# Fused attention, feed-forward and routed experts on one core: the first expert's gather split by the last tile, the last routes moved ahead, six experts ranked instead of five

## The chip, the cores and the metric

One core of a Trainium2 chip. The metric is the device time of one execution in microseconds. PE is the matrix engine, DVE the VectorE, ACT the ScalarE, POOL the GpSimd, SP the engine that issues most DMAs.

## What is computed

```python
attn_out = _attn_ref(...)             # q, k, v: 4 x 12 x 448 x 64, q and k normalised
x = attn_out.transpose(0, 2, 1, 3).reshape(1792, 768)
h = x @ w_in                          # 768 -> 2048
x = (max(h, 0) + alpha * min(h, 0)) @ w_out          # 2048 -> 768
do_compute = x @ w_skip > 0           # second stage: 8 experts, one per token
e_idx = argmax(x @ w_gate); gate_w = softmax(x @ w_gate)[e_idx]
for e in range(8):                    # w1[e]: 768 x 1024, w2[e]: 1024 x 768
    y[e_idx == e] = gate_w * (max(x @ w1[e], 0) @ w2[e])
out = x; out[do_compute] += y
```

## The kernel before

Every product is made of float16 pairs (a high and a low part: three products stand for one), so each float32 matrix that comes from DRAM is cut into a high half (ACT, line 1394) and a low half (DVE, line 1401, or POOL, lines 1404 and 1408).

**Stages.** Attention runs over 24 pairs of heads. Its rows go into blocks of tokens (two 128-token tiles in most, one in block 1 and in the last, block 7); `layer1` makes 2048 columns of a block (lines 1028 to 1030), `layer2` brings them back to 768 (lines 1116 to 1118), copies a tile out of PSUM as `zt` (line 1133) and writes it to `out` (line 1155) and to the DRAM buffer `zd` (line 1158). Each tile's router scores pick an expert; `route` counts and gives each token a slot of its expert. The scores of a tile come out of nine more columns of layer 2, or out of `logits_apart` (line 1231). When the last tile is routed, `all_slots` has for each expert the list of its token rows.

**Experts.** An expert's pass has a fixed number of slots, its entry in `WIDTHS`. The first `FIXED` experts have one by their number; the others are ranked by their counts on the chip, and the expert of a rank gets that rank's width. `fetch` gathers an expert's rows out of `zd` by an indirect DMA on POOL (line 1460), in two parts (128 rows and the rest) where the width is over 128; `turns` turns them on PE (line 1476) and cuts them (lines 1480 and 1483); `ups` and `downs` are the two products (lines 1443 to 1445); `backs` turns the result back (line 1524), adds it times the gate to the gathered rows (line 1530), and a scatter on POOL writes them to `out` (line 1536). `braid` lays the order of PE out by hand: up 0, up 1, down 0, up 2, down 1 and so on. Turns of expert e stand between the down products of expert e - 2, back turns of expert e between the up products of expert e + 2. Tokens beyond a width go to a loop at the end (line 1817), which runs zero times when all fit.

**Order and buffers.** The class `Plan` simulates the engines while the program is built: `op(key, (engine, ns, step), after, takes, uses)` gives a step its priority (lower first), its duration for the planner and its place in the order of its engine's queue. On the chip each queue keeps that order. A `buf` of a pool is a place; the takes of a pool go round its places in turn. Activations of the layers live in pool `x` (4 places), rows of the experts in `rows` (4 places).

**Weights of the experts.** 16 matrices of 1024 x 768, in 12 pieces of 256 KB (w1) or 8 of 384 KB (w2), each through a staging place. The first matrices are loaded during the layers; from `GATE` (matrix 4, piece 4) on a load waits for expert 0's gather. Before, seven staging places serve matrices 0 to 5, and eight the others. Of matrix 6 and later every fourth piece (`LO_G`) has its low half made by POOL in two steps, a scaling (line 1404) and a subtraction (line 1408).

Of the kernel before, what the change touches and what calls it, by code (L numbers as in the profile page):

```python
# [206 lines left out]
def attention_moe_routed_experts(  # L207
# [42 lines left out]
    FIXED = 3  # L250
    WIDTHS = [CAP] * FIXED + [CAP, 128, 96, 80, 64]
# [8 lines left out]
    zd = dram.tile([NT, DM], F32, name="zd")  # L260
# [31 lines left out]
    big = ctx.enter_context(tc.tile_pool(name="big", bufs=4))  # L292
    gp = es_l.enter_context(tc.tile_pool(name="gp", bufs=1))
    xp = es_l.enter_context(tc.tile_pool(name="xp", bufs=N_X))
# [58 lines left out]

    def late_constants():

        make_identity(nc, ident)
# [10 lines left out]
        V.tensor_copy(tokz, tokz_i)  # L367
        pref_i = stage.tile([128, NE], I32, tag="st", name="pref_i")
# [640 lines left out]

    def layer1(blk, prev):  # L1010
# [5 lines left out]
        gs = slice(AT_G[blk], AT_G[blk] + size)  # L1016
        for m0 in range(0, KF, step):
            b_h, b_gf = buf("h"), buf("gf")
            w = {}
            for m in range(m0, m0 + step):  # L1020
                for x in range(2):
                    def mm(m=m, x=x, w=w, m0=m0):
# [11 lines left out]
                        20000 + 1000 * blk + m, ("T", 23 + 9 * size * 5 // 12, mm), takes=[b_h] if new else [],  # L1034
# [16 lines left out]
            def hi(e, w=w, at=at):  # L1051
                def f():
                    if e is A:
                        A.activation(g_h[:, at, gs], w["gf"], AF.Copy)  # L1054
                    else:
                        V.tensor_copy(g_h[:, at, gs], w["gf"])
                return f

            def lo(e, w=w, at=at):
                def f():  # L1060
                    e.tensor_tensor(g_l[:, at, gs], w["gf"], g_h[:, at, gs], op=ALU.subtract)  # L1061
# [21 lines left out]
    lgs, n_kept = {}, []  # L1083
    lgz = const.tile([128, sum(SIZES_B[:Z_LOGITS]) // 128, NL], F32, name="lgz") if Z_LOGITS else None

    def layer2(blk, done, apart, early):
# [4 lines left out]
        if early:  # L1091
            for s in range(tiles):
                n = logits_apart(t0 + s, s, done, key)
# [5 lines left out]
        for s, half, g in todo:  # L1099
            tt = t0 + s  # L1100
            if g == 0 and half == 0:
                zt[s] = ({}, buf("zt1"))
# [6 lines left out]
            def mm(g=g, w=w, half=half, n=n, s=s):  # L1109
# [4 lines left out]
                for kk in range(4 * g, 4 * g + 4):  # L1114
                    gh, gl = (x[:, kk, AT_G[blk] + s * 128:AT_G[blk] + (s + 1) * 128] for x in (g_h, g_l))
# [7 lines left out]
                + ([n_router] if n > HD else []),  # L1123
# [6 lines left out]
            def z_out(w=w, half=half):  # L1130
                if half == 0:
                    w["zt"] = ztp.tile([128, DM], F32, tag="zt", name="zt")
# [6 lines left out]
            w["n_out"] = n_out  # L1139
            if half == 0:  # L1140
# [16 lines left out]
            def keep(w=w, tt=tt):  # L1157
                Y.dma_start(out=zd[tt * 128:(tt + 1) * 128, :], in_=w["zt"])
# [61 lines left out]
    def logits_apart(tt, s, done, key):  # L1220
        b_z = buf("z")
        w = {}
        o = AT_G[FROM_B.index(128 * tt)] if 128 * tt in FROM_B else 128 * s

        def mm():
# [3 lines left out]
            for kk in range(KF):  # L1229
                gh, gl = (x[:, kk, o:o + 128] for x in (g_h, g_l))  # L1230
# [13 lines left out]
    counted = [None, None]  # L1244

    def route(tt, n, late=[]):
# [30 lines left out]
        def position():  # L1277
# [6 lines left out]
            lgs[tt]["sel"] = sel  # L1284

# [40 lines left out]
        counted.append(n8)  # L1326

    reads = {}
    for blk in range(NB):
        done = layer1(blk, reads)  # L1330
        read = layer2(blk, done, blk < max(1, Z_LOGITS) or blk == NB - 1, blk == NB - 1)
        for x in range(AT_G[blk], AT_G[blk] + SIZES_B[blk], 128):
            reads.update({(x, g): n for g, n in read.items()})
# [19 lines left out]
    uses = sorted([(e, x) for e in range(NE) for x in range(2)], key=lambda u: 2 * u[0] + LAG * u[1])  # L1353
    b_w, n_w, w_ready, gates = {}, [None], {}, [None]

    def matrix_place(i, pool, name):

        u = uses[i]
# [9 lines left out]
    def matrix_steps(i, first=0, last=None):  # L1368

        e, second = u = uses[i]  # L1370
# [8 lines left out]
        for x, (src, at, n) in list(enumerate(expert_pieces(second, rows)))[first:last]:  # L1379
            got["pieces"] = got.get("pieces", -1) + 1  # L1380
            own = PLACES[got["pieces"] % (len(PLACES) if i >= 6 else 7)]
# [21 lines left out]
            def lo_scale(w=w, n=n):  # L1403
                G.tensor_tensor(w["st"], w["st"], sixteen.to_broadcast([128, n]), op=ALU.mult)
# [26 lines left out]
            if x % LO_G == LO_G - 1 and i >= 6:  # L1431
                n3 = op(key - 0.25, ("G", 1001 if small_ else 1428, lo_scale), uses=[b_st], after=[n2])
# [14 lines left out]
    class Pass:  # L1447
# [9 lines left out]
        def gather(self, x):  # L1457
            n, gi, si, gt = self.parts[x]
            r = self.pools["rows"].tile([128, DM], F32, tag=f"rows{x}", name="rows")
            G.indirect_dma_start(  # L1460
                out=r[0:n, :], out_offset=None, in_=zd, in_offset=bass.IndirectOffsetOnAxis(ap=gi, axis=0)
# [85 lines left out]
        def fetch(self, e):  # L1547

            k0 = 30000 + 1000 * e
            self.b_rows = [buf(f"rows{x}") for x in range(len(self.parts))]  # L1550
            self.moved = [1092 * p[0] // 128 for p in self.parts]
            self.n_g = [
                op(
                    k0 - 800, ("G", (1040, n), lambda x=x: self.gather(x)), takes=[self.b_rows[x]],
                    after=n_kept + [n_slots, n_ranked if e >= FIXED else None], dma=True,
                )
                for x, n in enumerate(self.moved)
            ]
# [55 lines left out]
        def backs(self, e):  # L1614
            k0 = 30000 + 1000 * e
            last = yield
            for x, moved in enumerate(self.moved):
                ns = []
                for half in range(2):
# [7 lines left out]
                        after=[n0],  # L1627
# [46 lines left out]
    nwin = const.tile([128, 1], I32, name="nwin")  # L1674

# [4 lines left out]
    def all_slots():  # L1680
        slots(table1, 128, gidx1, sidx1, gate1, all1)
        slots(table2, cap2, gidx2, sidx2, gate2, all2)

# [70 lines left out]
    with tc.manual_schedule():  # L1754
# [5 lines left out]
        got["st2"] = es_e.enter_context(tc.tile_pool(name="st2", bufs=4, side="right"))  # L1760
        plan.pool("st2", 4)
# [6 lines left out]
        plan.run(first)  # L1768
        plan.ahead, plan.tail = AHEAD2, TAIL2

        es_ps.close()
        es_l.close()
        got["st3"] = es_e.enter_context(tc.tile_pool(name="st3", bufs=N_ST3))
        plan.pool("st3", N_ST3)
        NBUF2 = dict(rows=4, zt=1, ht=2, yt=1) if LAG > 1 else dict(rows=3, zt=1, ht=1, yt=1)
        pools = {n: es_e.enter_context(tc.tile_pool(name=n, bufs=NBUF2[n])) for n in NBUF2}
        pools["ps_t"] = psum(es_e, "t", 4)
        pools["ps_h"] = psum(es_e, "h2", 4)
        for n, b in dict(NBUF2, rows0=NBUF2["rows"], rows1=NBUF2["rows"], t=4, h2=4).items():
            plan.pool(n, b)  # L1780
        ps = []
        for e in range(NE):
# [7 lines left out]
            ps.append(Pass(pools, parts, True))  # L1790
            ps[e].fetch(e)
        gates[0] = ps[0].n_g[-1]
# [3 lines left out]
        last = braid(None, ps[0].turns(0))  # L1796
# [12 lines left out]
        braid(last, ps[-1].backs(NE - 1))  # L1809
        plan.run()  # L1810
# [103 lines left out]
```

## Time and profile before

| what | us |
|---|---|
| median of three runs | 994.85 (991.01 to 997.11) |
| the profiled execution | 991.68 |
| its span, first to last instruction | 989.9 |
| PE, DVE, ACT, POOL busy | 819.5, 694.2, 572.6, 362.3 |

The profiled execution is 1.8 us longer than its span, and 3.2 us under the median. Its page shows busy time by engine; the stage in question is the last quarter, from the end of the layers on.

### The profile page before, as it was taken

The page shows a single profiled execution, that of the slowest core. Times are in us where ns is not written, and L with a number is a line of the kernel's source. Part 1 is how long each engine was busy: PE and PEld are TensorE (multiplying, and loading weights), DVE is VectorE, ACT ScalarE, POOL GpSimd, SP SyncE. Part 2 cuts the span into 40 slices and gives each one's busy share as a digit, 9 for nine tenths or more (in the row PEclk, how much of TensorE's full clock was granted, in tenths as well). Part 3 has the DMA queues.
Part 4 walks back from the last instruction along what each step waited for, and adds up shares of the span by engine and source line. Part 5 has one row for each costly group of instructions (what it writes and reads, how often), then busy time and mean ns, then how long its engine had stood idle before and what let it go on. Part 6 is the DMA issues. An engine that isn't in the chain of part 4 may idle for free. (4 is left out here: it accounts for less than half of the span.)

```text
span 989.9 us, 22385 instructions
## 1 busy us (share of the span) xinstructions
PE 819.5 (83%) x8325; PEld 597.1 (60%) x8325; DVE 694.2 (70%) x1611; ACT 572.6 (58%) x1298; POOL 362.3 (37%) x567
## 2 busy tenths in 40 slices
PE   2334448985988998999999899999999859999896
PEld 1213226772545565655665577677686628999896
DVE  6978887798658667888888668242323566889982
ACT  5777887788656665556676556121122336666661
POOL 3545574446325134342332001000101131476893
PEclk9955559986989999999999999999999978999999
DMA  6798988989999999779778956110104458877871
GB/s 187 195 192 201 228 205 174 215 211 213 179 218 191 200 196 187 154 157 171 158 146 169 157 126 223 33 32 29 37 1 161 148 165 303 264 246 254 282 259 34
DMA packets 272834, 170.72 MB, mean 172 GB/s; under 512 B 226086, under 2 KB 239526, under 8 KB 272720
## 3 DMA queue, kind: packets, MB, share of 16 engines
q1 hardware_dynamic: 270464, 161.86, 69.0%
q0 software_dynamic: 1536, 5.42, 1.7%
q10 hardware_dynamic: 720, 1.97, 0.7%
q8 instruction: 67, 1.10, 0.5%
q14 instruction: 47, 0.39, 0.1%
HBM read 100.91 MB, written 14.30 MB: 116 GB/s over the span
## 5 line engine op out<-in xcount | busy, mean ns | idle before, releaser
L1028 PE MATMUL hp<-xh,win 128*128 128x256 f16 (+1 forms) x768 | 193.9, 263 | 3.0 <-DVE gf L1047 3.0
L1029 PE MATMUL hp<-xl,win 128*128 128x256 f16 (+1 forms) x768 | 193.3, 262 | 0.0
L1030 PE MATMUL hp<-xh,win 128*128 128x256 f16 (+1 forms) x768 | 193.2, 262 | 0.0
L1116 PE MATMUL zp<-wout,g_h 128*128 128x384 f16 (+1 forms) x448 | 149.6, 334 | 4.6 <-ACT g_h L1054 2.6
L1118 PE MATMUL zp<-wout,g_l 128*128 128x384 f16 (+1 forms) x448 | 149.0, 333 | 0.4 <-DVE g_l L1061 0.4
L1117 PE MATMUL zp<-wout,g_h 128*128 128x384 f16 (+1 forms) x448 | 148.8, 332 | 0.0
L1401 DVE SCALAR_TENSOR_TENSOR we<-ew,we 128x512 f16<-128x512 f32 (+1 forms) x136 | 133.9, 1026 | 13.6 <-ACT we L1394 13.2
L911 DVE SCALAR_TENSOR_TENSOR p<-sp,r,p 128x448 f16<-128x448 f32 x168 | 111.0, 679 | 37.9 <-ACT p L905 37.0
L890 ACT ACTIVATE sp<-sp,m 128x448 f32<-128x448 f32 x168 | 102.0, 609 | 50.1 <-DVE m L884 48.6
L877 PE MATMUL sp<-qkT 64*64 64x448 f16 (+1 forms) x672 | 92.6, 417 | 45.3 <-DVE p L911 21.9
L905 ACT ACTIVATE p<-sp,r 128x448 f16<-128x448 f32 x168 | 103.2, 636 | 44.9 <-DMA pt<-p 19.5
L1394 ACT ACTIVATE we<-ew 128x512 f16<-128x512 f32 (+1 forms) x158 | 106.1, 710 | 25.5 <-DMA ew<-in_moe_w_dram 21.9
L884 DVE TENSOR_REDUCE m<-sp 128x2 f32<-128x896 f32 x96 | 92.7, 968 | 18.8 <-PE sp L877 18.5
L1047 DVE SCALAR_TENSOR_TENSOR gf<-gf,oma,hp 128x256 f32<-128x256 f32 (+1 forms) x128 | 50.5, 441 | 63.6 <-ACT gf L1043 63.5
L1028 PEld LDWEIGHTS <-win 128*128 128x128 f16 x768 | 76.0, 99 | 27.6 <-issue 12.9
L877 PEld LDWEIGHTS <-qkT 64*64 64x64 f16 (+1 forms) x672 | 28.4, 117 | 91.2 <-issue 67.8
L1029 PEld LDWEIGHTS <-win 128*128 128x128 f16 x768 | 76.1, 99 | 9.3
L1030 PEld LDWEIGHTS <-win 128*128 128x128 f16 x768 | 76.1, 99 | 6.9
L1445 PEld LDWEIGHTS <-we 128*128 128x128 f16 x768 | 75.6, 100 | 7.4 <-issue 7.4
L1444 PE MATMUL hp<-zl,we 128*128 128x176 f16 (+4 forms) x384 | 71.6, 228 | 6.8 <-DVE zl L1483 6.7
L1061 POOL TENSOR_TENSOR g_l<-gf,g_h 128x512 f16<-128x512 f32 x24 | 32.7, 1361 | 120.7 <-ACT g_h L1054 114.3
L1443 PEld LDWEIGHTS <-we 128*128 128x128 f16 x768 | 75.6, 100 | 0.7
(225 smaller groups left out, 1860.6 us busy)
## 6 DMA issues: line engine op xcount, KB each, us to landing
ew<-in_moe_w_dram SPq DMA_DIRECT2D x96, 256.0 KB, 4.1
ew<-in_moe_w_dram SPq DMA_DIRECT2D x64, 384.0 KB, 5.4
st<-in_moe_w_out_dram SPq DMA_DIRECT2D x31, 384.0 KB, 4.0
st<-in_moe_w_in_dram SPq DMA_DIRECT2D x28, 384.0 KB, 3.8
qk<-in_k_dram SPq DMA_DIRECT2D x24, 224.0 KB, 3.5
qk<-in_q_dram SPq DMA_DIRECT2D x24, 224.0 KB, 3.3
vf<-in_v_dram SPq DMA_DIRECT2D x24, 224.0 KB, 3.7
zd<-zt SPq DMA_DIRECT2D x14, 384.0 KB, 2.8
```

The costliest lines, as they stand in the source:

```text
L877: T.matmul(out=sp[r, j, 0:S].rearrange("p (j c) -> p j c", j=NJ), lhsT=qT[:, r], rhs=kT[:, :, r], start=(x == 0), stop=(x == last),)
L890: A.activation(e, e, AF.Exp, bias=w["m"][:, x:x + 1], scale=1.0, accum_out=w["s"][:, x, S:S + 1])
L905: A.activation(w["p"][:, x, 0, :], w["s"][:, x, 0:S], AF.Copy, scale=w["r"][:, x:x + 1])
L911: V.scalar_tensor_tensor(p[:, 1, :], w["s"][:, x, 0:S], w["r"][:, x:x + 1], p[:, 0, :], op0=ALU.mult, op1=ALU.subtract)
L1028: T.matmul(out=o, lhsT=win(0, c, m), rhs=xh[:, c, :], start=(c == 0), stop=False)
L1029: T.matmul(out=o, lhsT=win(0, c, m), rhs=xl[:, c, :], start=False, stop=False)
L1030: T.matmul(out=o, lhsT=win(1, c, m), rhs=xh[:, c, :], start=False, stop=(c == KD - 1))
L1116: T.matmul(out=zp, lhsT=gh, rhs=wout(0, kk, ws), start=(kk == 0), stop=False)
L1117: T.matmul(out=zp, lhsT=gh, rhs=wout(1, kk, ws), start=False, stop=False)
L1118: T.matmul(out=zp, lhsT=gl, rhs=wout(0, kk, ws), start=False, stop=(kk == KF - 1))
L1394: A.activation(o, w["st"], AF.Copy, scale=SC_W)
L1401: V.scalar_tensor_tensor(l, w["st"], SC_W, h, op0=ALU.mult, op1=ALU.subtract)
```

## The change

The last block's layer 1 is done before layer 2 of the block ahead of it, into tiles of its own, so that the router scores of the last three tiles come before their layer 2. The gather of expert 0 takes the rows of all tiles but the last: its row numbers are cut off at the number of a row of zeros, which is written to `zd` ahead of the last tile's rows (these move by one). A 0/1 matrix (`last_sel`) adds the last tile's rows on PE, out of `zt`, to the turned ones. Expert 0's rows are gathered a second time, whole, for the sum at the end. `FIXED` falls from 3 to 2: six experts are ranked, with one more width of 64. Rows share the four places of pool `x`; staging has three places for matrices 0 to 5 and seven later, the matrices of the two fixed experts are loaded first, POOL's share of the low halves is every third piece, and the scaling ahead of it moves to ACT.

```diff
-    FIXED = 3
-    WIDTHS = [CAP] * FIXED + [CAP, 128, 96, 80, 64]
+    FIXED = 2
+    WIDTHS = [CAP] * FIXED + [CAP, 128, 96, 80, 64, 64]
...
-    XFER, TAIL2, N_ST3, UP2 = 1150, 3500, 1, 2740
-    GATE, LO_G = (4, 4), 4
-    PLACES = ["st2", "st", "st2", "st", "st2", "st", "st2"] + ["st3"] * N_ST3
+    XFER, TAIL2, N_ST3, UP2 = 1150, 3500, 3, 2740
+    GATE, LO_G = (4, 0), 3
+    PLACES = ["st", "st3", "st", "st3", "st", "st3", "st4"]
...
+        key1 = 20000 + 1000 * blk if blk < NB - 1 else 20000 + 1000 * (blk - 1) + 50
...
+                + ([n_router] if n > HD else []) + ([l1_done[-1]] if blk == NB - 2 else []),
...
+                V.tensor_scalar(last_sel, iota_f, poss[:, tt:tt + 1], own, op0=ALU.is_equal, op1=ALU.mult)
...
+        if blk < NB - 1:
+            dones[blk] = layer1(blk, reads)
+        if blk == NB - 2:
+            dones[NB - 1] = layer1(NB - 1, {})
+        done = dones[blk]
+        read = layer2(blk, done, blk < max(1, Z_LOGITS) or blk >= NB - 2, blk >= NB - 2)
...
+    loads = sorted(uses, key=lambda u: u[0] >= FIXED)
...
-            own = PLACES[got["pieces"] % (len(PLACES) if i >= 6 else 7)]
+            own = PLACES[got["pieces"] % (len(PLACES) if i >= 6 else 1)]
...
-            def lo_scale(w=w, n=n):
-                G.tensor_tensor(w["st"], w["st"], sixteen.to_broadcast([128, n]), op=ALU.mult)
+            def lo_scale(w=w):
+                A.activation(w["st"], w["st"], AF.Copy, scale=SC_W)
...
+        def fetch_early(self):
...
+                    after=n_kept[:-1] + [n_slots, n_z] + n_g[-1:],
...
+            def tile_rows(c):
+                for j in range(2):
+                    T.matmul(
+                        out=own[c][:, j, 0:n], lhsT=last_rows["w"]["zt"][:, (c + j) * 128:(c + j + 1) * 128],
+                        rhs=last_sel[:, 0:n], start=False, stop=True,
+                    )
...
+                n1 = step1(
+                    20000 + 1000 * NB - 40, ("T", 600, lambda c=c: tile_rows(c)), uses=[b_s, last_rows["b"]],
+                    after=[n0, last_rows[0], n_placed[-1]] + ([last_rows[1]] if c else []),
+                )
...
+        def fetch_again(self):
+            b = buf("x")
+            self.b_rows, self.n_g = [b, b], []
+            for x, n in enumerate(self.moved):
+                self.n_g.append(op(
+                    30400, ("G", (1040, n), lambda x=x: self.gather(x)), takes=[] if x else [b],
+                    uses=[b] if x else [], dma=True, after=n_kept + [self.n_turned] + self.n_g[-1:],
+                ))
...
-        gates[0] = ps[0].n_g[-1]
+        ps[0].fetch_again()
+        gates[0] = n_kept[-1]
```

## Rows read from the trace of the kernel before

**Rows 1.** Stretches: length, then PE, PEld, DVE, ACT, POOL busy, PEclk, DMA share, GB/s.
```profile
802.32:817.42 15.10, 4.08 (x12) 2.17 (x13) 8.88 (x36) 3.61 (x6) 8.98 (x8) 0.64 0.53 158
...
982.81:989.87 7.06, 0.00 (x1) 0.00 (x0) 0.74 (x3) 0.00 (x0) 0.93 (x1) 0.82 0.05 12
```

**Rows 2.** Waits of PE from 735 us on: us in total, times, longest.
```profile
PE zp L1476 <- DMA rows<-zd,gidx: 11.0, 2, 10.4
PE hp L1444 <- DVE zl L1483: 6.7, 4, 2.5
PE zp L1116 <- ACT g_h L1054: 2.6, 1, 2.6
PE lgp L1231 <- ACT zt L1133: 0.6, 1, 0.6
```

**Rows 3.** PE in order of time: start, length, line, operation, [idle before].
```profile
801.82 0.33 PE L1117 MATMUL zp<-wout,g_h 128*128 128x384 f16 x1
801.99 0.33 PE L1118 MATMUL zp<-wout,g_l 128*128 128x384 f16 x1
...
812.75 0.45 PE L1476 MATMUL zp<-ident,rows 128*128 128x128 f32 x1 [10.44 <-DMA rows<-zd,gidx]
...
817.42 0.33 PE L1443 MATMUL hp<-zh,we 128*128 128x176 f16 x1
```

**Rows 4.** SP's queue in order of time; x is the number of DMAs.
```profile
589.88 19.27 SPq L1388 DMA_DIRECT2D ew<-in_moe_w_dram  x24
...
802.87 0.33 SPq L1158 DMA_DIRECT2D zd<-zt  x1
...
818.37 145.97 SPq L1388 DMA_DIRECT2D ew<-in_moe_w_dram  x112
```

**Rows 5.** Down products of 176, 128, 96, 80, 64 columns: PE, ACT, PEclk, DMA, GB/s.
```profile
856.35:860.00 3.65, 3.65 (x48) 0.00 (x0) 1.00 0.77 208
946.54:949.22 2.68, 2.68 (x49) 0.38 (x1) 1.00 1.02 349
963.10:965.14 2.04, 2.04 (x48) 0.31 (x1) 1.00 0.25 44
971.70:976.86 5.16, 5.16 (x144) 0.61 (x2) 1.00 0.14 40
977.67:981.87 4.20, 4.20 (x144) 0.56 (x2) 1.00 0.16 42
```

**Rows 6.** PE in order of time, turns of a column pair at full clock.
```profile
846.52 0.91 PE L1476 MATMUL zp<-ident,rows 128*128 128x128 f32 x4
```

**Rows 7.** POOL in order of time, two gathers.
```profile
806.30 3.39 POOL L1460 DMA_INDIRECT rows<-zd,gidx  x1 [9.96 <-DMA out_dram<-zt]
...
904.35 1.31 POOL L1460 DMA_INDIRECT rows<-zd,gidx  x1 [0.30 <-issue]
```

**Rows 8.** ACT in order of time, the last copy of a tile.
```profile
802.35 0.49 ACT L1133 ACTIVATE zt<-zp 128x384 f32<-128x384 f32 x1 [3.34 <-PE zp L1118]
```

**Rows 9.** PE in order of time, first turns of expert 4.
```profile
898.14 0.38 PE L1476 MATMUL zp<-ident,rows 128*128 128x128 f32 x2
```

**Rows 10.** DMA issues from 589.8 to 590 us: KB each, us to landing.
```profile
ew<-in_moe_w_dram SPq DMA_DIRECT2D x1, 256.0 KB, 2.6
```

**Rows 11.** Groups by form, 818 us to the end: xcount, busy, mean ns, idle before.
```profile
L1401 DVE SCALAR_TENSOR_TENSOR we<-ew,we 128x512 f16<-128x512 f32 x48 | 48.1, 1052 | 2.2 <-ACT we L1394 2.1
...
L1394 ACT ACTIVATE we<-ew 128x768 f16<-128x768 f32 x52 | 42.6, 839 | 12.9 <-DMA ew<-in_moe_w_dram 12.5
L1394 ACT ACTIVATE we<-ew 128x512 f16<-128x512 f32 x58 | 34.0, 626 | 6.2 <-DMA ew<-in_moe_w_dram 6.0
...
L1404 POOL TENSOR_TENSOR ew<-ew,sixteen 128x512 f32<-128x512 f32 x12 | 14.2, 1186 | 18.8 <-ACT we L1394 18.7
```

**Rows 12.** DVE in order of time, a low half while POOL is idle.
```profile
792.22 0.68 DVE L1401 SCALAR_TENSOR_TENSOR we<-ew,we 128x512 f16<-128x512 f32 x1
```

**Rows 13.** Waits of SP's queue, 818 us to the end.
```profile
SPq L1388 <- POOL we L1408: 37.9, 17, 4.4
```

More of the change, by code (lines that the diff above doesn't have):

```diff
@@ L1139, in layer2 @@
             w["n_out"] = n_out
+            if tt == NTT - 1:
+                last_rows.update({"w": w, "b": b_zt, half: n_out})
             if half == 0:
@@ L1222, in logits_apart @@
         w = {}
-        o = AT_G[FROM_B.index(128 * tt)] if 128 * tt in FROM_B else 128 * s
+        blk = max(x for x in range(NB) if FROM_B[x] <= 128 * tt)
         def mm():
@@ L1284, in position @@
             lgs[tt]["sel"] = sel
+            if tt == NTT - 1:
+                own = small.tile([128, 1], F32, tag="own0", name="own0")
+                V.tensor_copy(own, hot[:, 0:1])
+                V.tensor_scalar(last_sel, iota_f, poss[:, tt:tt + 1], own, op0=ALU.is_equal, op1=ALU.mult)
         def weight():
@@ L1368, in matrix_steps @@
     def matrix_steps(i, first=0, last=None):
-        e, second = u = uses[i]
+        e, second = u = loads[i]
         n_new = n_w[i + 1]
@@ L1455, in __init__, with gather @@
             self.rows, self.hp, self.yp = {}, {}, {}
-        def gather(self, x):
+        def gather(self, x, early=None):
             n, gi, si, gt = self.parts[x]
-            r = self.pools["rows"].tile([128, DM], F32, tag=f"rows{x}", name="rows")
+            r = xp.tile([128, DM], F32, tag=("xh", "xl")[x], name="rows")
+            gi, src = (gi, zd) if early is None else (early, zd[0:NT - 127, :])
             G.indirect_dma_start(
-                out=r[0:n, :], out_offset=None, in_=zd, in_offset=bass.IndirectOffsetOnAxis(ap=gi, axis=0)
+                out=r[0:n, :], out_offset=None, in_=src, in_offset=bass.IndirectOffsetOnAxis(ap=gi, axis=0)
             )
@@ L1549, in fetch @@
             k0 = 30000 + 1000 * e
-            self.b_rows = [buf(f"rows{x}") for x in range(len(self.parts))]
+            b = buf("x")
+            self.b_rows = [b for x in self.parts]
             self.moved = [1092 * p[0] // 128 for p in self.parts]
[L1552 to L1555, printed above, removed]
-                )
-                for x, n in enumerate(self.moved)
-            ]
+            self.n_g = []
@@ L1674, in attention_moe_routed_experts @@
     nwin = const.tile([128, 1], I32, name="nwin")
+    early1, early2 = (const.tile([128, 1], I32, name=n) for n in ("early1", "early2"))
     def total():
@@ L1759, in attention_moe_routed_experts @@
         plan.pool("we", 2)
-        got["st2"] = es_e.enter_context(tc.tile_pool(name="st2", bufs=4, side="right"))
-        plan.pool("st2", 4)
+        es_g = ExitStack()
+        last_g = es_g.enter_context(tc.tile_pool(name="last_g", bufs=1, side="right"))
+        for n in ("g_h", "g_l"):
+            got[n] = last_g.tile([128, KF, SIZES_B[-1]], F16, name="last_" + n)
         plan.ahead = AHEAD1
@@ L1767, in attention_moe_routed_experts @@
         matrix_steps(GATE[0], 0, GATE[1])
[L1768 to L1780, printed above, removed]
+        pools = {}
         ps = []
@@ L1790, in attention_moe_routed_experts @@
             ps.append(Pass(pools, parts, True))
+        ps[0].fetch_early()
+        plan.run(first)
+        plan.ahead, plan.tail = AHEAD2, TAIL2
+        es_ps.close()
+        es_l.close()
+        es_g.close()
+        got["st3"] = es_e.enter_context(tc.tile_pool(name="st3", bufs=N_ST3, side="right"))
+        plan.pool("st3", N_ST3)
+        got["st4"] = es_e.enter_context(tc.tile_pool(name="st4", bufs=1))
+        plan.pool("st4", 1)
+        NBUF2 = dict(zt=1, ht=2, yt=1)
+        pools.update((n, es_e.enter_context(tc.tile_pool(name=n, bufs=NBUF2[n]))) for n in NBUF2)
+        pools["ps_t"] = psum(es_e, "t", 4)
+        pools["ps_h"] = psum(es_e, "h2", 4)
+        for n, b in dict(NBUF2, t=4, h2=4).items():
+            plan.pool(n, b)
+        for e in range(1, NE):
             ps[e].fetch(e)
-        gates[0] = ps[0].n_g[-1]
+        ps[0].fetch_again()
+        gates[0] = n_kept[-1]
         matrix_steps(GATE[0], GATE[1])
@@ L1795, in attention_moe_routed_experts @@
             matrix_steps(i)
-        last = braid(None, ps[0].turns(0))
+        last = None
         for i, (e, second) in enumerate(uses):
```

119 lines of the change are left out of this document (95 added, 24 removed).

## The prediction

> **What bounds the kernel now.** I read the busy table by stage first, then the matrix engine's (PE's) list of waits, then the time lines of PE and of the queues that feed it. From 740 us on PE has one hole that matters: the stretch from its last layer-2 product at 802.32 to the first expert product at 817.42, 15.1 us long, in which it is busy for 4.08 us at a mean granted clock of 0.64 (between its levels of 1.2 and 2.4 GHz) [rows 1]. The list of waits names the reason: 11.0 us for the first expert's gathered rows; all other waits of PE from 735 us to the end are short, 6.7 us for the low halves of turned rows and 2.6 and 0.6 us at the end of layer 1 [rows 2, 3]. The reader is to see a chain: last tile out, its rows written to DRAM, gather, turning, first product. After 817.42 PE hardly stops until 982.81, and the last scatter's 7.06 us follow [rows 1]. So two things set the end: that hole, and 165.4 us of expert products. Behind the products stands a third: the weights. Their last load is issued at 964.34 [rows 4], 13.3 us ahead of the last expert's second product at 977.67 [rows 5]; they were close to being late.
>
> **The change part by part.** T0 is the end of PE's last layer-2 product (802.32 before). Last expert product and its back turns end at T0 + 180.5 before.
>
> *Layer 1 of the last block ahead of layer 2 of the block before it, routes of three tiles early.* PE's products are the same but for two more separate router products, each 48 narrow matmuls; at the narrowest cadence seen, 4.20 us for 144 [rows 5], 1.4 us each: +2.8. The turning of the early rows (two of three column pairs) and one product with the last tile fall before T0 too: 0.9 us each by the four turns in 0.91 us [rows 6], +2.7. The holes of 2.6 and 0.6 us go [rows 2], but layer 2 then has no layer-1 work to fill the change of its single accumulator: six changes at 0.6, 3.6. The turns fit into some of these holes: I take 3 us back. Sum: T0 moves by 2.8 + 2.7 - 3.2 + 3.6 - 3 = +2.9, say 3 us (bounds 0 and +6).
>
> *The gather of expert 0 without the last tile.* Before, rows were ready 10.4 us after T0 [rows 3]: write issued at 802.87 [rows 4], gather begun at 806.30 [rows 7], turned from 812.75. The same chain now starts from the tile before, 16 us earlier (96 products of 384 columns, one each 0.165 us) [rows 3], and so has some 5 us to spare. What stays behind T0 is the last half tile's copy, 0.49 us, begun 0.03 after the product [rows 8], and two products with the 0/1 matrix. No f32 product that isn't a turn stands in the trace; the nearest are turns, 0.9 us for the four of a column pair at full clock [rows 6] and 4.08/3 = 1.36 at the low one [rows 1]. I take the first, nearer in clock: 0.5 + 2 x 0.9 = 2.3 us (bounds 2 to 4). The hole of 15.1 becomes 3 + 2.3 = 5.3: **-9.8 us** (bounds -14 and -5). The second gather for expert 0 (its rows are wanted whole for the sum at the end) adds two issues on POOL; they are needed only at the back turns 40 us later. The zero row with its DMA, the shifted token numbers and the few small VectorE instructions for the 0/1 matrix lie beside layer-1 and layer-2 products: nothing, and a few tenths of a us each without that cover.
>
> *Six experts ranked.* Widths go from 176 x4, 128, 96, 80, 64 to 176 x3, 128, 96, 80, 64 x2. A pass is 288 matmuls; their cadence is 76.0, 55.8, 42.5, 35.8 and 29.2 ns [rows 5], so a pass costs 21.9, 16.1, 12.2, 10.3 or 8.4 us. Sum before 134.6, after 121.1: **-13.5 us** of PE, all of it in the later experts. If an expert's tokens don't fit its place, the window loop runs and loads every expert again; the reference's own inputs (155, 107, 80, 162, 52, 62, 65, 8 tokens) fit both ways.
>
> *Row buffers.* Rows now rotate through four buffers of the former activations, and expert 0 takes its place a second time. In the order of the takes expert 4 gets the buffer of expert 1, where before it got that of expert 0. Expert 1's rows leave only after its back turns, which stand between the up products of expert 3; expert 4's turning stands right behind them. Before, these back turns end at 898.14, where expert 4's turns begin [rows 9]; the gather that waited for expert 1's scatter is issued at 904.35 for 1.31 us [rows 7]. A gather lands some 3.1 us after its issue's end (812.75 - 806.30 - 3.39) [rows 3, 7], so expert 4's rows would come at 908.7, 10.6 us late, with everything on PE queued behind them: **+11 us** (bounds 0 and +13, the upper with some time at the low clock).
>
> *Weights.* Before, 112 pieces from 818.37 on, 145.97 us [rows 4]: 1.30 us each. Now the fixed experts alone are loaded ahead and 120 pieces remain, from T0 + 4 on (the time from T0 to the gather's start, which waited for the same write). The first 24 go through three staging places instead of seven. Three places turn over once per landing (2.6 us alone) [rows 10], high half 0.63, low half 0.68 to 1.05 [rows 11, 12] and some 0.5 of hand-offs: 4.4 to 4.8 us, 1.6 us a piece (bounds 0.80, the 24 pieces in 19.27 us through seven places [rows 4], and 2.2 with landings 2 us longer). The other 96 use seven places, a third of the low halves on POOL, which loses its scaling (1.19 us) to ACT at 0.63 [rows 11]. ACT then has 12 x 0.63 + 8 x 0.84 + 4 x 0.63 + 2 x 0.84 = 18.5 us for an expert's 20 pieces and some 4 us of evictions: 1.12 a piece. POOL was the engine for which the load queue waited longest, 37.9 us [rows 13], and that wait shortens. I take 1.15 (bounds 0.99, the 0.80 above by bytes, and 1.30 as before). End: 3 + 4 + 24 x 1.6 + 96 x 1.15 + 7 for the last piece's landing and conversion + 5.2 for the last expert's product and turns = T0 + 168.0.
>
> The Trainium skill, "DMA: Bandwidth & Descriptors", section on the anatomy of one DMA, gives a DMA (there one issued by GpSimd; these come from SP) a fixed 2.0 us plus its bytes over 436 GB/s: estimate 2.6 us for 256 KB, of which a short rotation hides little. The lone landing agrees, and by it three places are too few: it speaks against this edit. With the 0.80 us of the 24 pieces in its place the weights would end 19 us earlier and PE alone would set the end; with the rule the sum stands as it is. The Trainium skill, "SBUF — State Buffer", section on the two sides, says that VectorE with two SBUF inputs and a reading GpSimd lock each other out for a whole instruction. The low half at 1.05 us beside POOL against 0.68 without it [rows 11, 12] agrees; by it the move of the scaling to ACT shortens VectorE's share as well, and the rate would lie nearer to 0.99, with PE alone setting the end at the same T0 + 168.2.
>
> **The sum.** By PE: 5.3 + 165.4 - 13.5 + 11 = T0 + 168.2; by the weights T0 + 168.0. Against 180.5 that is -12.3 us, so 991.68 - 12.3 = 979.4 for the profiled execution. That one lies 3.2 us below the median; on the median's scale 982.6, and I say 982.5.
>
> **Rivals.** *A, both gains whole:* the rows of expert 4 come in time (if the takes fall in another order) and the weights keep up; PE alone sets the end, 11 us less: 971.5. For it speaks that PE waited for no weight before; against it the order of the four buffers. *B, the weights become the bound, slower:* with three staging places at 2.2 us a piece and the old rate, 3 + 4 + 52.8 + 124.8 + 12.2 = 196.8, 16 us more than before: 1011; with 1.6 and 1.30 it is 182.4, near 997. At 1.6 us for the first 24 it decides at 1.28 us for the others: above it the kernel is slower than before. For it: the load queue was never free before, and ACT gets fuller. Against it: 24 pieces took 0.80 us each where the engines had room. *C, the change doesn't do what it says:* the early gather sits behind other work on POOL, or the write of the tile before behind weight loads on SP, and the hole stays; -13.5 + 11 + 3 gives 995.
>
> **How the numbers follow.** Forecast 0.45 (own range 974 to 991), A 0.2, B 0.2, C 0.13, an overflow of a narrower place 0.02. About 1% (9.9 us) is what a measurement here can tell from no change: faster is under 984.9, slower over 1004.8. Faster: two thirds of the forecast, all of A, a little of C: 0.54. Slower: half of B and the overflow: 0.12. The rest, 0.34, lies between. The range runs from 967, below A, to 1000, which leaves out the worse half of B.
>
> **What would show it.** The wait of PE for gathered rows after the last layer-2 product is gone, and expert products start some 5 us after 802 instead of 15. A new wait of about 10 us stands ahead of expert 4's turns; if it is missing, A. Products of 64 columns come twice. If PE waits for weights (for the low halves on VectorE or POOL) in the experts of 96 columns and below, the third term was too small; the load queue's rate (pieces by time) says by which of the two prices. A start of the expert products later than T0 + 10 makes C right.

## The result, and the profile after

The changed kernel takes 1003.15 us (median of 12 runs, 1000.22 to 1006.91), the kernel before, beside it, 995.2 (12 runs): the ratio is 1.0082, 95% interval 1.006 to 1.0103. It is slower by 8 us where 12 us less were forecast. The profiled execution after takes 1003.78 us (span 1002.1) and is typical of its median; that of before, 991.68, was 3.5 us quicker than its median on this chip. So the two traces lie 12.1 us apart, of which 8 are the kernels'.

The stretches of the changed kernel: from a `zd` write during layer 2 to T0, from T0 to the first expert product, the expert products, and the last scatter. Columns are length, then PE, PEld, DVE, ACT, POOL busy, PEclk, DMA share, GB/s.
```profile
716.70:811.83 95.13, 88.98 (x897) 65.52 (x895) 46.83 (x184) 26.75 (x47) 4.93 (x8) 0.98 0.33 98
811.83:814.39 2.56, 2.56 (x17) 2.16 (x17) 0.00 (x0) 0.89 (x2) 0.00 (x0) 1.00 0.47 173
814.39:995.26 180.87, 151.65 (x2426) 145.22 (x2423) 126.65 (x184) 111.84 (x211) 64.97 (x50) 0.89 0.74 241
995.26:1002.10 6.84, 0.01 (x1) 0.00 (x0) 0.74 (x3) 0.00 (x0) 0.90 (x1) 0.79 0.05 12
```
The first stretch and the third of the kernel before, by the same view:
```profile
713.90:802.32 88.42, 84.64 (x779) 60.14 (x776) 40.65 (x154) 26.51 (x51) 6.96 (x6) 0.96 0.36 117
...
817.42:982.81 165.39, 158.36 (x2437) 153.03 (x2436) 132.31 (x167) 99.03 (x188) 101.48 (x65) 0.97 0.74 244
```
Read together with [rows 1]: T0, the end of PE's last layer-2 product, comes 9.5 us later (811.83 for 802.32), the hole falls from 15.10 to 2.56, the expert products take 180.87 for 165.39, the tail is the same. 9.5 - 12.5 + 15.5 - 0.2 = 12.3, the distance of the two spans but for rounding. The hole was won as forecast. What the kernel lost lies in the expert products, in which PE is now busy for *fewer* us (151.65 for 158.36): they got narrower, and PE waits. Its waits from 735 us on, to be laid beside [rows 2]:
```profile
PE zp L1512 <- DVE we L1431: 11.7, 1, 11.7
PE hp L1480 <- POOL we L1443: 4.6, 2, 2.9
PE yp L1480 <- DVE we L1436: 3.7, 3, 2.8
PE lgp L1252 <- ACT zt L1151: 3.1, 1, 3.1
PE yp L1478 <- DVE hl L1537: 2.8, 2, 2.1
...
PE yp L1480 <- POOL we L1443: 2.0, 1, 2.0
PE yp L1478 <- ACT we L1429: 1.4, 2, 1.1
```
The wait of 11.0 us for the first rows is gone. A single wait of 11.7 us is new, and after it come waits for halves of weights (`we`), which PE never had before. The time line of PE shows the closed hole and, 88 us later, the turns of expert 4 behind the new wait; these rows answer [rows 3] and [rows 9]:
```profile
811.50 0.33 PE L1133 MATMUL zp<-wout,last_g_l 128*128 128x384 f16 x1
811.66 1.50 PE L1630 MATMUL ezp<-ident,rows 128*128 128x128 f32 x8
813.09 1.46 PE L1638 MATMUL ezp<-last_sel,zt 128*128 128x176 f32 x8
814.39 0.24 PE L1478 MATMUL hp<-zh,we 128*128 128x176 f16 x1
...
902.13 0.55 PE L1512 MATMUL zp<-ident,rows 96*128 96x96 f32 x2 [11.70 <-DVE we L1431]
```
The list names VectorE for that wait, but POOL's time line shows what it was: expert 1's scatter at 892.46, behind it two subtractions, then the gather of expert 4 and that of expert 5. The first waits for nothing but its place in the queue (0.16 us, "issue") and lands 5.9 us after its start, at 902.0, as PE goes on (answers [rows 7]).
```profile
892.46 1.16 POOL L1572 DMA_INDIRECT out_dram<-rows,sidx  x1 [2.23 <-DVE rows L1566]
893.64 2.27 POOL L1443 TENSOR_TENSOR we<-ew,we 128x512 f16<-128x512 f32 x2
896.07 1.21 POOL L1496 DMA_INDIRECT rows<-zd,gidx  x1 [0.16 <-issue]
897.58 0.91 POOL L1496 DMA_INDIRECT rows<-zd,gidx  x1 [0.30 <-issue]
```
```profile
rows<-zd,gidx POOLq DMA_INDIRECT x1, 5.9
```
SP's queue, the first 20 pieces and all 120 (answers [rows 4], where 112 took 145.97):
```profile
818.62 28.19 SPq L1423 DMA_DIRECT2D ew<-in_moe_w_dram  x20
...
818.62 164.90 SPq L1423 DMA_DIRECT2D ew<-in_moe_w_dram  x120
```
The first 20 pieces of before, by the same view, were issued in 18.36 us:
```profile
818.37 18.36 SPq L1388 DMA_DIRECT2D ew<-in_moe_w_dram  x20
```
The last load is issued at 983.52, and PE ends 11.7 us later: the weights end last now. (That this is the same number as the wait ahead of expert 4 is chance.)

### The profile page after: what moved, and what is told of

Its sections match the earlier page's. It is cut to its first block, busy times and chain, and to the rows that moved or that the text cites. A ratio compares the mean times of both kernels' runs of the same rounds, so it can differ in the third digit from the quotient of the medians.

```text
span 1002.1 us, 22615 instructions
## 1 busy us (share of the span) xinstructions
PE 817.8 (82%) x8433; PEld 595.6 (59%) x8433; DVE 684.3 (68%) x1626; ACT 584.4 (58%) x1312; POOL 312.9 (31%) x546
## 5 line engine op out<-in xcount | busy, mean ns | idle before, releaser
L1041 PE MATMUL hp<-xh,win 128*128 128x256 f16 (+1 forms) x768 | 190.5, 260 | 2.5 <-DVE gf L1060 2.5
L1042 PE MATMUL hp<-xl,win 128*128 128x256 f16 (+1 forms) x768 | 189.9, 259 | 0.0
L1043 PE MATMUL hp<-xh,win 128*128 128x256 f16 (+1 forms) x768 | 189.9, 259 | 0.0
L1436 DVE SCALAR_TENSOR_TENSOR we<-ew,we 128x512 f16<-128x512 f32 (+1 forms) x132 | 120.3, 931 | 42.5 <-ACT we L1429 41.6
L1131 PE MATMUL zp<-wout,g_h 128*128 128x384 f16 (+1 forms) x416 | 138.9, 334 | 4.0 <-ACT zt L1151 2.5
L1133 PE MATMUL zp<-wout,g_l 128*128 128x384 f16 (+1 forms) x416 | 138.2, 332 | 0.7 <-POOL g_l L1075 0.7
L1132 PE MATMUL zp<-wout,g_h 128*128 128x384 f16 (+1 forms) x416 | 138.3, 332 | 0.0
L1429 ACT ACTIVATE we<-ew 128x512 f16<-128x512 f32 (+1 forms) x144 | 100.8, 715 | 52.7 <-DMA ew<-in_moe_w_dram 51.7
L1041 PEld LDWEIGHTS <-win 128*128 128x128 f16 x768 | 75.0, 98 | 25.0 <-issue 12.4
L1480 PEld LDWEIGHTS <-we 128*128 128x128 f16 x768 | 77.8, 103 | 13.8 <-POOL we L1443 7.0
L1478 PEld LDWEIGHTS <-we 128*128 128x128 f16 x768 | 77.8, 103 | 5.5 <-DVE hl L1537 3.1
L1042 PEld LDWEIGHTS <-win 128*128 128x128 f16 x768 | 75.2, 98 | 8.0
L1043 PEld LDWEIGHTS <-win 128*128 128x128 f16 x768 | 75.2, 98 | 6.6
L1479 PEld LDWEIGHTS <-we 128*128 128x128 f16 x768 | 77.8, 103 | 0.3
L1480 PE MATMUL yp<-hh,we 128*128 128x176 f16 (+4 forms) x384 | 68.2, 228 | 5.6 <-DVE we L1436 3.7
```

The costliest lines, as they stand in the source:

```text
L1041: T.matmul(out=o, lhsT=win(0, c, m), rhs=xh[:, c, :], start=(c == 0), stop=False)
L1042: T.matmul(out=o, lhsT=win(0, c, m), rhs=xl[:, c, :], start=False, stop=False)
L1043: T.matmul(out=o, lhsT=win(1, c, m), rhs=xh[:, c, :], start=False, stop=(c == KD - 1))
L1131: T.matmul(out=zp, lhsT=gh, rhs=wout(0, kk, ws), start=(kk == 0), stop=False)
L1132: T.matmul(out=zp, lhsT=gh, rhs=wout(1, kk, ws), start=False, stop=False)
L1133: T.matmul(out=zp, lhsT=gl, rhs=wout(0, kk, ws), start=False, stop=(kk == KF - 1))
```

## The experiments

Two theories at the start. **W**: the path of the weights (transfer, staging place, conversions) runs too slowly by itself and sets the end. **S**: the order of the queues is fixed; conversions stand behind evictions of PE's results in ACT's and VectorE's queues, so PE's new wait delays the weights, and they are late only for that. All runs are set against runs of the kernel before on the same chip (994.31 us in the first four, 991.55 in the next four, 992.34 in the last); ratios are comparable, times only within a few us. The loads (first issue to last) and PE's end are those of the one profiled execution, which lies up to 4.7 us off its median (y1).

| run | us | ratio, 95% | loads, us | PE ends |
|---|---|---|---|---|
| changed kernel | 1003.15 | 1.0082 (1.006 to 1.0103) | 164.90 | 995.26 |
| x1_again_first | 1007.94 | 1.0136 (1.0075 to 1.0196) | 166.98 | 999.64 |
| x2_seven_places | 987.2 | 0.9931 (0.9899 to 0.9963) | 146.06 | 979.14 |
| x3_both | 993.03 | 0.9981 (0.9952 to 1.001) | 149.29 | 988.82 |
| x5_tail | 995.89 | 1.0033 (0.9994 to 1.0071) | 156.92 | 983.94 |
| y1_widths | 1004.29 | 1.0115 (1.0072 to 1.0157) | 169.41 | 1000.57 |
| y2_places_widths | 998.74 | 1.0089 (1.0066 to 1.0112) | 150.44 | 987.96 |
| y3_eight_places | 989.08 | 0.9975 (0.995 to 1.0) | 146.08 | 976.83 |
| y4_scale_pool | 1000.49 | 1.009 (1.0067 to 1.0114) | 155.59 | 992.60 |
| z1_half_bytes | 977.61 | 0.9889 (0.9792 to 0.9985) | 139.54 | 965.41 |
| z2_half_lows | 977.93 | 0.9882 (0.9797 to 0.9967) | 141.56 | 969.48 |
| z3_places_tail | 990.03 | 0.9991 (0.9949 to 1.0033) | 147.10 | 983.04 |
| z4_eight_tail | 980.68 | 0.99 (0.9862 to 0.9939) | 138.16 | 968.75 |

**x1_again_first**: expert 0's second gather gets its place in pool `x` earlier, so that expert 4 doesn't need expert 1's buffer.
```diff
-                    30400, ("G", (1040, n), lambda x=x: self.gather(x)), takes=[] if x else [b],
+                    30100, ("G", (1040, n), lambda x=x: self.gather(x)), takes=[] if x else [b],
```


> The changed kernel with one key altered: the second gather for expert 0 goes ahead of expert 1's, so that expert 4's rows take the buffer of expert 0 and not of expert 1. Theory S (the loads' conversions stand on ACT and VectorE in a fixed order between the evictions of PE's products, so a PE wait holds up the weights too): the wait of 11.7 us ahead of expert 4's turns goes, the last load is issued 8 to 10 us earlier, and the time falls by 8 to 11 us, to about 993. Theory W (the load path runs on its own and alone sets the end): the wait goes, but PE then waits as much longer for weights in experts 5 to 7, and the time stays within 3 us of 1003.

The wait ahead of expert 4 is gone and nothing is won: 0.5% over the changed kernel by the ratios, with intervals that overlap. All but 1.5 us of PE's waits from 815 us on are for weights now (six groups like these, 26.1 us):
```profile
PE yp L1480 <- DVE we L1436: 6.9, 7, 2.3
PE yp L1480 <- POOL we L1443: 5.9, 3, 2.5
...
```
The loads took 166.98 us without PE's wait: S falls in its plain form. The wait of 11.7 us was real, and in the changed kernel it cost nothing.

**x2_seven_places**: the 24 pieces of matrices 4 and 5 (the first matrices of experts 2 and 3, 12 pieces of 256 KB each) may use all seven staging places. The planner then lays out the queues anew.
```diff
-            own = PLACES[got["pieces"] % (len(PLACES) if i >= 6 else 1)]
+            own = PLACES[got["pieces"] % (len(PLACES) if i >= 4 else 1)]
```


> The changed kernel with the first 24 pieces after the gate through all seven staging places instead of three. Theory S: these pieces come sooner in the planned order, the rest of the loads stands earlier too, and the waits for weights in experts 5 to 7 (some 17 us) shrink by half or more; the wait for expert 4's rows stays; about 995. Theory W with the three places as the cause: the first 24 pieces take about 20 us instead of 30 and the last load is issued 10 us earlier; about 993. If the first 24 pieces are no cause, the time stays within 3 us of 1003.

1.5% quicker than the changed kernel by the ratios, 15 to 16 us, from one digit; both theories had said 993 to 995. SP's queue, and what PE waited for:
```profile
819.09 146.06 SPq L1423 DMA_DIRECT2D ew<-in_moe_w_dram  x120
```
```profile
PE zp L1512 <- DMA rows<-zd,gidx: 14.0, 1, 14.0
PE hp L1478 <- ACT zh L1516: 3.6, 1, 3.6
```
The waits for weights all but vanish (0.4 us); expert 4's wait is left. This comes nearest to the kernel that the prediction had described. Pieces 1 to 20 go out in 19.4 us instead of 27.9. In the changed kernel the 24 are through only with the 30th load, six of the next matrix (384 KB, seven places) going out between them; in x2 they are the first 24. The changed kernel (its queue, and these loads by size), then x2:
```profile
818.62 40.76 SPq L1423 DMA_DIRECT2D ew<-in_moe_w_dram  x30
ew<-in_moe_w_dram SPq DMA_DIRECT2D x24, 256.0 KB, 4.2
ew<-in_moe_w_dram SPq DMA_DIRECT2D x6, 384.0 KB, 5.4
```
```profile
819.09 22.49 SPq L1423 DMA_DIRECT2D ew<-in_moe_w_dram  x24
```

**x3_both**: x1 and x2 together.


> Both edits together: second gather for expert 0 first, seven places for the first 24 pieces. Theory S: both gains add, 982 to 988. Theory W: the gain is that of the places alone, about 993.

Not the sum of both, and W's 993. Expert 4's wait is gone and the weights are late again: 1.24 us a piece, and PE waits some 16 us for them. In x2 the two chains end almost together (the last load's issue and 12 us give 977.2, PE ends at 979.1), so removing PE's wait shows the other.

**x5_tail**: only one number of the planner, how long after its transfer a DMA lands in its simulation, and so only how it lays out the queues.
```diff
-    XFER, TAIL2, N_ST3, UP2 = 1150, 3500, 3, 2740
+    XFER, TAIL2, N_ST3, UP2 = 1150, 1500, 3, 2740
```


> The changed kernel with one number of the planner altered: it believes that a DMA lands 1.5 us instead of 3.5 us after its transfer. No instruction changes, only the order in the queues of the expert stage. Theory S: conversions stand earlier between the evictions, the loads run faster (under 1.30 us a piece against 1.37) and the time falls by 4 to 12 us. Theory W: places and durations are the same, so the rate of the loads and the time stay within 3 us; slower only if ACT or VectorE now wait for DMAs ahead of evictions.

The loads are 8 us shorter (1.31 us a piece, where S had said under 1.30), and the time falls by 0.5% by the ratios, with intervals that just overlap. No operation is added or left out, but more than the order of conversions and evictions changes: the loads go out in another order too, and the planner, which picks the engine of each high half, gives VectorE 20 of them behind T0 for 16 (ACT 100 for 104). So something of S is right: how the queues are laid out matters, beside the places. The run doesn't say which part of the layout does.

**y1_widths** and **y2_places_widths**: the old widths, put back into the changed kernel and into x2.
```diff
-    WIDTHS = [CAP] * FIXED + [CAP, 128, 96, 80, 64, 64]
+    WIDTHS = [CAP] * FIXED + [CAP, CAP, 128, 96, 80, 64]
```


> Undoes only the narrower widths: expert 3 takes the full CAP again and the five after it the old 128, 96, 80, 64 columns in order (the sixth expert's ranking bound is left where it is). By the moving columns of the prediction this is 13.5 us more PE work. Theory W (the 120 pieces of weights, at 1.37 us each, end after the PE would have): the added columns run in the gaps in which PE waits for weights, so the time rises by 0 to 4 us over the changed kernel's 1003, the loads keep their 165 us, and the gaps of PE for weights shrink by some 10 us. Theory S (PE's order sets the end and weights only look late because conversions stand behind PE's evictions): the time rises by the whole 10 to 14 us, to 1013 to 1017, and the loads stretch with it, to 175 us or more.

> The kernel with all seven places for pieces from expert 3's on, with the old widths put back as well. There the loads took 146 us and PE waited for no weights, so PE should bound it. Theory W: the widths are now worth what their columns cost, so 9 to 14 us over the 987 of seven places alone, 996 to 1001. If the widths were never worth anything, 987 to 990.

In the changed kernel the wider columns cost 0.3% (3 us, within the intervals), and PE's waits for weights shrink from 11.7 to 6.1 us: the columns run in the waits. In x2 they cost 1.6% (some 16 us, by the intervals 12 to 20). The narrower widths are worth what the prediction said (13.5), and the changed kernel threw it away because PE didn't set its end.

**y3_eight_places**: x3 with an eighth place.
```diff
-    XFER, TAIL2, N_ST3, UP2 = 1150, 3500, 3, 2740
+    XFER, TAIL2, N_ST3, UP2 = 1150, 3500, 4, 2740
...
-    PLACES = ["st", "st3", "st", "st3", "st", "st3", "st4"]
+    PLACES = ["st", "st3", "st", "st3", "st", "st3", "st4", "st3"]
```


> Seven places from expert 3's pieces on, expert 4's rows fetched before the first expert's products (no wait ahead of its turns), and an eighth place for pieces (a fourth buffer of the second ring). With seven places and the early fetch alone the loads took 149 us, PE waited some 15 us for weights, and the time was 993. If the number of places limits the pieces, the loads fall to 140 us or less and the time to 982 to 988. If the rate of conversions, or the order in which they stand between PE's evictions, limits them, the loads stay within 4 us of 149 and the time within 990 to 995.

The ratio is x3's, and the loads are 146 us (x3: 149): beyond seven, places aren't what is short. The trace shows what the pieces wait for instead. ACT, then VectorE, in order of time:
```profile
880.82 0.46 ACT L1549 ACTIVATE y<-yp 128x352 f32<-128x352 f32 x1 [3.12 <-PE yp L1478]
881.18 0.38 ACT L1514 ACTIVATE zh<-zp 128x256 f16<-128x256 f32 x1
884.68 0.47 ACT L1549 ACTIVATE y<-yp 128x352 f32<-128x352 f32 x1 [3.12 <-PE yp L1478]
886.69 0.38 ACT L1532 ACTIVATE hh<-hp 128x256 f16<-128x256 f32 x1 [1.54 <-PE hp L1478]
889.03 0.38 ACT L1532 ACTIVATE hh<-hp 128x256 f16<-128x256 f32 x1 [1.96 <-PE hp L1478]
889.31 1.66 ACT L1427 ACTIVATE we<-ew 128x512 f16<-128x512 f32 x3
```
```profile
887.03 0.62 DVE L1564 SCALAR_TENSOR_TENSOR rows<-bp,gate,rows 128x384 f32<-128x384 f32 x1 [5.01 <-PE bp L1558]
```
From 877 to 889 us ACT makes no high half: five evictions of PE's results stand first in its queue, four of which wait for PE, while VectorE stands 5.0 us before an addition that waits for back turns. Three conversions follow in a burst once the eviction at 889.03 is through. Pieces were there: the four loads issued from 872.79 to 874.53 landed some 4.7 us after their issue, and no engine made a high half from 876.9 to 889.3.
```profile
ew<-in_moe_w_dram SPq DMA_DIRECT2D x4, 256.0 KB, 4.7
```

**y4_scale_pool**: x2 with the scaling of the third low halves put back on POOL.
```diff
-            def lo_scale(w=w):
-                A.activation(w["st"], w["st"], AF.Copy, scale=SC_W)
+            def lo_scale(w=w, n=n):
+                G.tensor_tensor(w["st"], w["st"], sixteen.to_broadcast([128, n]), op=ALU.mult)
```


> Seven places, and the scaling of each piece's low half put back from ACT to POOL, as a product with a constant. POOL would carry it at some 1.0 to 1.4 us a piece beside the gathers and scatters, ACT would be 0.63 to 0.84 us a piece freer. If ACT's queue is what holds the pieces, the loads shorten by 5 to 10 us against 146 and the time stays at 985 to 988, since PE set the end there. If POOL's is, the loads lengthen to 155 us or more and the time rises to 992 to 1000.

Slower than x2 by 1.6%: POOL, not ACT, is the fuller queue. (The planner also moves high halves back to ACT, 117 for 101 in x2.) PE's two longest waits are both for POOL, for its gathers (14.0 us of that in x2 too) and for one of its low halves:
```profile
PE zp L1512 <- DMA rows<-zd,gidx: 19.2, 4, 15.2
PE yp L1480 <- POOL we L1443: 3.7, 1, 3.7
```
With seven places, the move of the scaling to ACT is a gain of the change.

**z1_half_bytes**: y3, but of the last 119 pieces only half is loaded; the conversions read that half twice. The second halves of the weights are left out, and the scaling on ACT takes two instructions for one.
```diff
-                Y.dma_start(out=w["st"], in_=src())
+                Y.dma_start(out=w["st"][:, 0:m], in_=src()[:, 0:m])
...
```


> The kernel with eight places and the early fetch for expert 4, in which the weights set the end (loads 146 us, 1.22 us a piece, some 14 us of PE's waits for weights), with each of the last 119 pieces loaded only half: the conversions read the loaded half twice, so their instructions keep their sizes and the second halves of the weights are left out of the result. Theory T (the transfers set the 1.22 us): the loads fall towards 110 us, PE's waits for weights go, and the time falls by 8 to 14 us to 976 to 981. Theory D (the conversions, VectorE's above all, or their order set it): the loads stay within 5 us of 146 and the time within 986 to 990.

**z2_half_lows**: y3, with VectorE's low half without its subtraction.
```diff
-                V.scalar_tensor_tensor(l, w["st"], SC_W, h, op0=ALU.mult, op1=ALU.subtract)
+                V.tensor_scalar(l, w["st"], SC_W, None, op0=ALU.mult)
```


> The same kernel with eight places, with the low half on VectorE made by a one-input scaling in place of the scaling and subtraction (the subtraction of the high half is left out, so the low halves are wrong by it); the instruction has the same elements and one SBUF input less, and should take some 0.6 us instead of 0.9 to 1.1. Theory D (VectorE's conversions set the 1.22 us a piece): the loads fall to 130 us or less, PE's waits for weights shrink under 5 us, and the time falls to 975 to 981. Theory T (the transfers set it): the loads stay within 5 us of 146, the time at 986 to 990.

Stretches of the loads in y3, z1 and z2:
```profile
817.60:963.70 146.10, 129.65 (x2106) 124.57 (x2104) 121.11 (x178) 101.21 (x194) 61.59 (x44) 0.95 0.85 283
```
```profile
813.60:953.10 139.50, 128.29 (x2103) 123.71 (x2102) 117.84 (x178) 103.76 (x222) 62.79 (x44) 0.95 0.56 168
```
```profile
814.80:956.30 141.50, 128.50 (x2107) 124.39 (x2106) 85.95 (x178) 98.40 (x191) 54.87 (x43) 0.96 0.87 291
```
Half the bytes (283 to 168 GB/s) shorten the loads by 6.6 us, a VectorE relieved of 35 us (121.11 to 85.95) by 4.6. Neither theory T nor D got its loads (110, 130), yet both times fell into the ranges. They are some 0.9% under y3 by the ratios, but the intervals overlap, so that a gain over y3 isn't shown; the loads are of one execution each. Neither the bandwidth nor VectorE's work sets the pace alone. That the two hold it together, each where the other is taken away, no run excludes.

**z3_places_tail** and **z4_eight_tail**: x5's number of the planner in x2 and in y3 (the diff is x5's).


> Seven places from expert 3's pieces on, and the planner's due time of late work at 1500 in place of 3500 (the order of the queues alone). With three places that order shortened the loads by 8 us and the time by 7. If the fixed order is still what the loads lose by, they fall from 146 to 140 us or less and the time stays at 984 to 988, since PE with its wait for expert 4's rows sets the end; if order and places had been the same loss, the loads stay at 144 to 148 us.

> Eight places, the early fetch for expert 4 and the due time of late work at 1500: here the weights set the end (1.22 us a piece, 989), so an order that loads faster shows in the time. If the fixed order costs the loads: 138 to 142 us and 980 to 985. If it doesn't: 146 us and 987 to 991.

In z3 no gain, as forecast for a kernel in which PE with its wait (16.9 us here) sets the end; but the loads don't shorten either (147.10 for 146.06), as the expectation had it for the case that order and places had been the same loss. In z4 the loads fall to 138.16 us (816.06 to 954.22) and the time to 0.99 of the kernel before, clear of the noise against that kernel and against y3: all operations as in y3, laid out otherwise (two more high halves on VectorE, 22 for 20). It has the lowest ratio of the versions that leave nothing out, 1.8% under the changed kernel; x2's interval overlaps its own.

## Why the prediction was wrong

Its sum had two chains, PE's and the weights', that tied at T0 + 168. Here is the weights' chain, counted like there from T0 of before, 802.32; the measured pieces are counted from the rows of SP's queue.

| term | predicted | measured |
|---|---|---|
| T0 moves | 3 | 9.5 |
| T0 to the first load | 4 | 6.8 |
| first 24 pieces | 24 x 1.6 = 38.4 | 32.8 |
| other 96 pieces | 96 x 1.15 = 110.4 | 132.1 (1.38 each) |
| last landing, conversion, product, turns | 12.2 | 11.7 |
| sum | 168.0 | 192.9 |

The pieces are counted as they were issued. Of the first 24, five are not pieces of the three places: the prediction had one group behind the other, and on the chip they mix.

**The step that failed** is the fourth, "the other 96 use seven places ... I take 1.15". It is rival B: 1.38 us a piece lies above its deciding point of 1.28 (and above the 1.30 given as the upper bound), and T0 + 192.9 between its 182.4 and 196.8. The text had named the waits for low halves that would show it, and they are there. Two things were wrong in it.

The first is the rate. The lower rows for it, 0.80 us a piece, came from a stretch in which the engines had no evictions of expert products between the conversions. Among them a piece costs more: behind the first 24, the other 96 cost 1.29 us each in x2 with seven places throughout (123.9 / 96) and 1.20 in the best layout (z4: 115.3 / 96). Even x2's is above the deciding point. For a better rate spoke that POOL was the engine for which the load queue waited longest, and that this wait shortens [rows 13]. It did, but the next row of that view, which the prediction didn't weigh, was as long, and grew. Before, then after:
```profile
SPq L1388 <- DVE we L1401: 36.6, 40, 4.2
```
```profile
SPq L1423 <- DVE we L1436: 56.4, 45, 4.3
SPq L1423 <- POOL we L1443: 24.8, 15, 6.0
```
ACT's sum of 1.12 us a piece had all high halves on ACT, too; the planner gave 16 of the 120 to VectorE.

The second is that the three places do harm beyond their own pieces. Those were priced about right: the 24 took 40.4 us for 38.4, with six others between them (22.2 in x2). But with the 32nd load, the same 32 pieces in both, the changed kernel is 11.6 us behind x2, and with the 40th 15.1. From 846.60 to 878.60 VectorE is busy for 22.36 us in the changed kernel (29.33 in x2, 847.10 to 879.10). By the 100th load 6 us are made up, and then the last 20 cost 35.4 (x2: 25.6; x5, three places in another layout: 27.6). Why those last pieces lose again under this layout, the runs don't separate. So the edit that was priced at 24 pieces by 1.6 us, and nothing after them, cost 15 to 16 us by x2 against the changed kernel, more than the gain of 12 that was forecast.

**The first load** comes 6.8 us behind T0 for 4. The 4 were the time to a gather's start, 3.2 here, but what opens the loads is a memset on POOL, and it stands in POOL's queue behind three gathers:
```profile
815.02 0.95 POOL L1496 DMA_INDIRECT rows<-zd,gidx  x1 [17.44 <-DMA zd<-zt]
...
818.47 0.12 POOL L1447 MEMSET ew<- 128x1 f32 x1
```

**T0**, the second miss: +9.5 for +3. Of it 2.9 were there at the `zd` write from which the first stretch is counted (716.78 after, 713.93 before), ahead of the work that moved, and lie within what executions differ by: in the versions above, which are like the changed kernel up to there, that write comes between 711.6 and 722.1. The 6.7 left are 4.3 of products (predicted 5.5) and 2.4 of holes (predicted 3.6 - 3.2 - 3 = -2.6): the 3 us that turns were to take back in the holes were not. That is a little past the upper bound of 6. The bound of -14 for the hole doesn't follow from its terms either (2 - 15.1 = -13.1), but has no part in the miss.

**What held.** The hole: 2.56 us for 2.3 behind T0, by the mechanism named. That the number is so near is luck: the third column pair's turns, which the sum had in no term behind T0, take 1.43 us there (811.66 to 813.09, as eight instructions, where a pair took four and 0.9 us before) and cover the copy, and the two products take 0.65 each for 0.9. Expert 4's wait: 11.7 us for 11, by the mechanism named (expert 1's scatter, then the gather). It cost nothing where the weights were later still (x1), and some 9 us where they weren't (z3 to z4, an eighth place being the other difference). The widths: 13.5 predicted, some 16 measured where PE sets the end (x2 to y2), 3 where it doesn't (y1). The Trainium skill, "SBUF — State Buffer", section on the two sides, was weighed for the scaling's move. VectorE's low half of 512 columns fell from 1052 ns [rows 11] to 918, and of 768 from 1270 to 1092, so the trace agrees in direction:
```profile
L1436 DVE SCALAR_TENSOR_TENSOR we<-ew,we 128x512 f16<-128x512 f32 x56 | 50.5, 918 | 14.3 <-ACT we L1429 13.9
L1436 DVE SCALAR_TENSOR_TENSOR we<-ew,we 128x768 f16<-128x768 f32 x35 | 38.0, 1092 | 11.6 <-ACT we L1429 11.4
```
With the scaling back on POOL they rise again, from 834 and 1211 ns in x2 to 953 and 1435 in y4. But what was concluded from that section, a rate nearer to 0.99, didn't follow, since VectorE's work alone isn't what sets the pace (z2). The rule of the Trainium skill, "DMA: Bandwidth & Descriptors", section on the anatomy of one DMA, spoke against the three places, and there it was right.

**What stays open**: how much of the pace of 1.20 to 1.29 is evictions ahead of conversions in the queues, how much the release of the places of the matrices by PE, and how much the engine picked for a high half; no run takes the evictions away, and every edit of places or of the planner moves all three.

## What to carry to other kernels

When two chains tie in a forecast, a term of either that is too cheap decides the sign: bound the rate of a load path by rows in which its engines also do the work that stands between (1.30 here), not by an empty stretch (0.80). A short rotation of staging places at the start of a long series can cost more than its own pieces: here the loads behind it were later still at the end. Before a wait is removed, ask which chain ends within a few us behind it: removing 11.7 us alone bought nothing here, and with the other chain mended, some 9.

## What the runs showed of the chip, unexpected

PE's waits cost more than their length, since products behind them run at the lower clock. Stretches of the changed kernel:
```profile
893.30:907.00 13.70, 4.87 (x33) 4.89 (x34) 11.87 (x10) 7.92 (x12) 7.94 (x7) 0.50 0.96 300
907.00:954.80 47.80, 42.66 (x847) 41.77 (x846) 39.86 (x59) 35.83 (x69) 21.84 (x16) 1.00 0.86 288
954.80:968.50 13.70, 8.48 (x123) 7.60 (x119) 11.42 (x18) 10.19 (x20) 4.34 (x3) 0.50 0.76 265
```
After the idle 11.70 us the granted clock stays at its lower level (0.50, 1.2 GHz) until 907.0, 4.9 us into the turns and products that follow, and it is there again for 13.7 us from the first waits for weights on; the full level (1.00) lies between. Half the bytes at an unchanged piece count moved the load rate by 5% only (z1: 1.22 to 1.16 us a piece, at a DMA share of 0.56 for 0.85). And with one SBUF input less, as another instruction, VectorE's low half falls from 794 ns (512 columns) and 1271 (768) in y3 to 477 and 739 in z2:
```profile
L1434 DVE TENSOR_SCALAR we<-ew 128x768 f16<-128x768 f32 x36 | 25.8, 739 | 2.0 <-DMA ew<-in_moe_w_dram 2.0
L1434 DVE TENSOR_SCALAR we<-ew 128x512 f16<-128x512 f32 x56 | 25.6, 477 | 8.6 <-DMA ew<-in_moe_w_dram 8.4
```
